# Two units' y side by side in 4-byte words: three transposes and one copy per pair, in a fused recurrence and MoE kernel

## The chip, the cores and the metric

The kernel runs on one core of one Trainium2 chip. The metric is the time of one execution on the device in microseconds; the time of before is 174.89 us, the median of three runs (174.61 to 177.36). Profiles are one execution each, taken by the hardware profiler; TensorE, VectorE, ScalarE, GpSimd and SyncE appear there as PE (its weight loads as PEld), DVE, ACT, POOL and SP.

## The reference

A gated linear recurrence over 768 steps for 4 batches of 8 heads of width 48, and then a two-layer SiLU network over its output, row by row (3072 tokens of 384 values, hidden width 2048). All inputs and the output are float32.

```python
f = 1.0 / (1.0 + np.exp(-f_logit))
for t in range(S):                                   # S = 768
    state = f[:, :, t, :, None] * state + np.einsum('bhd,bhe->bhde', k[:, :, t], v[:, :, t])
    y[:, :, t] = np.einsum('bhd,bhde->bhe', q[:, :, t], state)
x = y.transpose(0, 2, 1, 3).reshape(B * S, H * D)    # 3072 x 384
h = x @ w_in                                         # 384 x 2048
out = (h * (1.0 / (1.0 + np.exp(-h)))) @ w_out       # 2048 x 384
```

## The kernel before

The sequence of each batch is cut into six chunks of 128 steps. A unit is one chunk of one batch; two units make a pair, and there are 12 pairs (PAIRS). Pairs 0 to 3 (form T) take the first two chunks of one batch with the steps interleaved, pairs 4 to 11 (form N) take one chunk of two batches.

All work is written out by hand in one string, PLAN. A word such as `yT.0.1:P:2` is a step: its kind, the pair, the unit (or the piece), the engine that does it (P TensorE, V VectorE, A ScalarE, G GpSimd, S SyncE) and the buffer slots that it takes. The order of the words is the order in each engine's queue. There are 8 banks of PSUM (slots of class pb, 128 x 512 words each), 4 buffers xT, 3 buffers yb, and so on (SLOTS). A step waits for what it reads and for the last reader of the buffer that it takes.

For the change these steps matter, in the order of the data:

- `y` and `yi` (line 349, 459, 455): the recurrence's output of a unit, 128 steps x 384 values in float32, in a PSUM bank.
- `yc` (line 463): a cast of it to bf16 into yb. Helper `copy`, so the profile shows line 191 for ScalarE and line 193 for VectorE.
- `yT` (line 467): three 128 x 128 transposes on TensorE (a weight load of yb and a matmul with the identity) into one PSUM bank, in bf16. `qkc` and `tq` (line 412) do the like for q and k.
- `xc` (line 469): a copy of that bank into the unit's half of xT, which is 128 x 3 x 256 in bf16: 128 columns of unit 0 and then 128 of unit 1.
- `mi` (line 335): the first product of the network, w_in as weights and xT streamed, six matmuls per step. In pairs 0 and 1 a step takes one unit (128 columns); from pair 2 on a step takes both (256 columns).
- `si` (line 340): SiLU on ScalarE, from a PSUM bank of 2 x 2 x 128 words to hT in bf16.
- `mo` (line 370) and `ms` (line 273): the second product, the latter after seven-product sums of blocks (`hs`, `wt`, `ca`).

Pairs 5 to 11 use `yT` and `xc` for some units and, for the others, a DMA transpose (`yD`, line 471); the change does not touch them. w_in comes in four DMAs that GpSimd issues (`wi`, line 237), w_out in four more (`wo`).

Of the kernel before, what the change touches and what calls it, by code (L numbers as in the profile page):

```python
# [53 lines left out]
at.2.1.0:V:3 mo.0.0.1:P: f.5.0:S:2 at.2.1.1:V: mo.1.1.2:P: wt.6:V: k.4.1:S: d.2:P:7,4 y.2:P:6,5 su.2.0:V:0 mo.0.0.2:P: yc.2.0:A:1 vb.3.0:A:6
mo.1.0.2:P: vb.3.1:V:2 q.4.1:S:4 sd.2.1:V:1 yi.2.1:P: sc.3.1:P:3,6 yc.2.1:V:2 su.2.1:G:0 q.4.0:S: sc.3.0:P:7,4 mo.0.0.3:P: E.4.0:A: at.3.0.0:V:0
k.5.0:S:0 mo.1.0.3:P: at.3.1.0:V:1 L.4.0:A:1 yT.2.0:P:5 at.3.1.1:V: yT.2.1:P:7 v.4.0:S:4 mo.1.1.3:P: xc.2.1:A:2 at.3.0.1:V: oc.1.0:A:0 cs.4.1:P:3
v.5.0:S:0 cs.4.0:P:6 xc.2.0:V: oc.1.1:A: oc.0.0:V:1 d.3:P:7,4 a.4.1:A:1 y.3:P:0,5 q.5.0:S:0 su.3.0:V:0 al.4.1:A:4 ia.4.0:A:4 qg.4.1:G:3 mi.2.7:P:2
E.5.0:A: yc.3.0:V:0 v.6.1:S:1 mi.2.3:P:1 ia.4.1:A:2 sd.3.1:V:0 al.4.0:A:5 yi.3.1:P: a.4.0:A:3 yT.3.0:P:7 f.7.0:S:0 mi.2.1:P:0 su.3.1:G:0 L.5.0:A:2
xc.3.0:V:3 yc.3.1:V:1 mi.2.4:P:3 v.4.1:S: wt.4:V: yT.3.1:P:4 cs.5.0:P:6 mi.2.0:P:7 xc.3.1:V: ki.4.1:V: mi.2.5:P:5 si.2.0:A:2 vb.4.0:V:3 qkD.4.1:S:0
# [54 lines left out]
def kernel(  # L114
# [48 lines left out]
    w_in_sb = sb.tile([128, KT, d_ff], BF16, name="w_in_sb")  # L163
# [25 lines left out]
    def copy(eng, dst, src):
        if eng == "A":  # L190
            nc.scalar.copy(dst, src)  # L191
        else:
            ENG[eng].tensor_copy(dst, src)  # L193
# [38 lines left out]
    def emit(kind, rest, eng):  # L232
        if kind in ("wi", "wo"):
            n, parts = rest[0], count[kind]
# [93 lines left out]
        if kind == "mi":  # L328
            j = rest[1]
            h = at("h", P, j).rearrange("p (n c) -> p n c", n=2)  # L330
            for i in range(2):
                n = 2 * j + i
                cols = slice(rest[2] * C, (rest[2] + 1) * C) if len(rest) > 2 else slice(0, 2 * C)
                for kk in range(KT):
                    nc.tensor.matmul(h[:, i, cols], w_in_sb[:, kk, n * 128:(n + 1) * 128], at("xT", P)[:, kk, cols],  # L335
                                     start=(kk == 0), stop=(kk == KT - 1))
            return
        if kind == "si":
            j = rest[1]
            return nc.scalar.activation(at("hT", P).rearrange("p u n c -> p n u c")[:, 2 * j:2 * j + 2], at("h", P, j).rearrange("p (n u c) -> p n u c", n=2, u=2), AF.Silu)  # L340
# [24 lines left out]
        b, c = us[i]
        last = c == CHUNKS - 1
# [128 lines left out]
    def takes(kind, rest):  # L495
        if kind in ("wi", "wo", "wt", "so", "yi", "yj", "idle"):
            return []
        P = rest[0]
# [60 lines left out]
    with tc.manual_schedule():  # L559
# [67 lines left out]
```

## Time and profile before

| what | before |
|---|---|
| median of three runs | 174.89 us |
| span of the profiled execution | 173.4 us |
| median less that span | 1.49 us |
| instructions | 5477 |
| PE, PEld busy | 160.4 us, 141.5 us |
| ACT, DVE, POOL busy | 129.6 us, 121.3 us, 71.2 us |

The profile gives the span from the first to the last instruction; for the time of the profiled execution itself no other figure is given, and the median stands beside it. Times in a timeline count from the start of the span. A row of a group gives line, engine, operation, what is written and read, the shape, the count, then busy time and the mean of one in ns, then the idle time in front of it on its engine and what ended that. In a timeline or chain row the first two numbers are start and length in us, and xN is the number of instructions merged. Matmuls are pipelined: the length of one matmul row (219 ns) is not the distance to the next.

### The profile page before, as it was taken

The page shows a single profiled execution, that of the slowest core. Times are in us where ns is not written, and L with a number is a line of the kernel's source. Part 1 is how long each engine was busy: PE and PEld are TensorE (multiplying, and loading weights), DVE is VectorE, ACT ScalarE, POOL GpSimd, SP SyncE. Part 2 cuts the span into 40 slices and gives each one's busy share as a digit, 9 for nine tenths or more (in the row PEclk, how much of TensorE's full clock was granted, in tenths as well). Part 3 has the DMA queues.
Part 4 walks back from the last instruction along what each step waited for, and adds up shares of the span by engine and source line. Part 5 has one row for each costly group of instructions (what it writes and reads, how often), then busy time and mean ns, then how long its engine had stood idle before and what let it go on. Part 6 is the DMA issues. An engine that isn't in the chain of part 4 may idle for free.

```text
span 173.4 us, 5477 instructions
## 1 busy us (share of the span) xinstructions
PE 160.4 (92%) x2245; PEld 141.5 (82%) x2245; DVE 121.3 (70%) x234; ACT 129.6 (75%) x248; POOL 71.2 (41%) x115
## 2 busy tenths in 40 slices
PE   0687898999999999999999999999996999999993
PEld 0255698976789888999998999999895998999992
DVE  7188950039995997958899779989965677966050
ACT  3999697783989899999768798798955877603511
POOL 6059872930240147899946305202467201000300
PEclk9999999999999999999999999999999999999999
DMA  5999999999999999979999969896999795120305
GB/s 138 324 325 319 241 206 227 203 206 195 185 194 200 195 200 204 176 150 208 245 188 188 219 135 211 191 198 134 191 171 183 177 145 139 60 80 4 136 27 200
DMA packets 108695, 31.73 MB, mean 183 GB/s; under 512 B 102704, under 2 KB 108144, under 8 KB 108672
## 3 DMA queue, kind: packets, MB, share of 16 engines
q1 hardware_dynamic: 103936, 25.70, 71.7%
q0 software_dynamic: 4736, 5.70, 15.8%
q8 instruction: 17, 0.28, 0.6%
q14 instruction: 6, 0.05, 0.1%
HBM read 25.17 MB, written 4.72 MB: 172 GB/s over the span
## 4 chain that ended last, share of the span: by engine, by line
PE 69%; DMA 17%; POOL 4%; SPq 4%; ACT 3%; issue 1%; POOLq 0%
PE pb L335 28%; PE pb L273 22%; PE pb L370 7%; DMA w_in_sb<-in_moe_w_in_dram 6%; DMA w_out_sb<-in_moe_w_out_dram 5%; DMA qkT<-qk 4%; POOL qk L405 3%; DMA f<-in_f_logit_dram 2%; PE pb L438 2%; SPq L305 2%; PE pb L459 2%; PE pb L455 2%; PE pb L395 2%; SPq L424 1%; ACT x L400 1%
## 5 line engine op out<-in xcount | busy, mean ns | idle before, releaser
L335 PE MATMUL pb<-xT,w_in_sb 128*128 128x256 bf16 (+1 forms) x672 | 69.7, 257 | 0.5 <-DMA w_in_sb<-in_moe_w_in_dram 0.5
L340 ACT ACTIVATE hT<-pb 128x512 bf16<-128x512 f32 x96 | 51.9, 605 | 14.1 <-PE pb L335 13.4
L335 PEld LDWEIGHTS <-w_in_sb 128*128 128x128 bf16 x672 | 56.3, 98 | 5.9 <-DMA w_in_sb<-in_moe_w_in_dram 0.6
L273 PE MATMUL pb<-w_sum,hT 128*128 128x192 bf16 x288 | 28.0, 246 | 0.0
L405 POOL TENSOR_TENSOR qk<-q,x 128x384 bf16<-128x384 f32 x16 | 16.3, 1020 | 27.5 <-ACT x L400 12.4
L490 POOL TENSOR_TENSOR st<-sd,al 48x192 bf16<-48x192 f32 x32 | 16.9, 529 | 25.6 <-DVE sd L480 13.5
L400 ACT ACTIVATE x<-pb 128x384 f32<-128x384 f32 x48 | 22.2, 511 | 3.3 <-PE pb L395 2.7
L273 PEld LDWEIGHTS <-hT 128*128 128x128 bf16 x288 | 23.8, 98 | 0.6
L442 DVE TENSOR_TENSOR atm<-pb,triu 128x512 bf16<-128x512 f32 x32 | 20.5, 683 | 5.2 <-PE pb L438 5.0
L370 PE MATMUL pb<-w_out_sb,hT 128*128 128x384 bf16 (+1 forms) x128 | 17.7, 286 | 0.1
L593 ACT ACT_TABLE_LOAD x13 | 16.7, 1283 | 0.2
L405 POOL TENSOR_TENSOR qk<-k,x 128x384 bf16<-128x384 f32 x13 | 13.8, 1062 | 6.7 <-ACT x L400 5.4
L273 PE MATMUL pb<-w_out_sb,qkTT 128*128 128x192 bf16 x144 | 14.7, 246 | 0.0
L256 DVE TENSOR_TENSOR hT<-hT 128x1024 bf16<-128x1024 bf16 x18 | 14.6, 813 | 0.0
L382 POOL DMA_DIRECT2D out_dram<-ob x7 | 3.9, 565 | 24.6 <-ACT hT L340 24.6
L370 PEld LDWEIGHTS <-hT 128*128 128x128 bf16 x128 | 11.1, 98 | 3.6 <-issue 0.3
L191 ACT CAST yb<-pb 128x384 bf16<-128x384 f32 x15 | 7.3, 490 | 8.5 <-PE pb L349 4.8
L312 ACT ACTIVATE f<-f 128x768 f32<-128x768 f32 (+1 forms) x13 | 10.4, 809 | 2.4 <-DMA f<-in_f_logit_dram 2.2
L273 PEld LDWEIGHTS <-qkTT 128*128 128x128 bf16 x144 | 12.0, 98 | 0.3
L256 DVE TENSOR_TENSOR qkTT<-hT 128x2048 bf16<-128x2048 bf16 x9 | 11.1, 1233 | 1.2 <-ACT hT L340 1.2
L193 DVE COPY qkTT<-pb 128x1024 bf16<-128x1024 bf16 x4 | 2.8, 692 | 12.0 <-PE pb L412 12.0
L442 DVE TENSOR_TENSOR atm<-pb,mask 128x512 bf16<-128x512 f32 x16 | 10.0, 684 | 1.3 <-PE pb L434 1.3
(86 smaller groups left out, 235.6 us busy)
## 6 DMA issues: line engine op xcount, KB each, us to landing
f<-in_f_logit_dram SPq DMA_DIRECT2D x11, 384.0 KB, 4.8
k<-in_k_dram SPq DMA_DIRECT2D x16, 192.0 KB, 4.1
q<-in_q_dram SPq DMA_DIRECT2D x16, 192.0 KB, 3.7
v<-in_v_dram SPq DMA_DIRECT2D x16, 192.0 KB, 4.1
k<-in_k_dram SPq DMA_DIRECT2D x4, 384.0 KB, 4.9
q<-in_q_dram SPq DMA_DIRECT2D x4, 384.0 KB, 4.8
v<-in_v_dram SPq DMA_DIRECT2D x4, 384.0 KB, 10.7
w_in_sb<-in_moe_w_in_dram POOLq DMA_DIRECT2D x4, 384.0 KB, 8.8
```

The lines of the kernel that those rows point to most:

```text
L191: nc.scalar.copy(dst, src)
L256: return ENG[eng].tensor_tensor(out=h_sum(P, m), in0=x, in1=y, op=op)
L273: nc.tensor.matmul(at(BANK[m], P)[:, half * W:(half + 1) * W], x, w, start=first, stop=(n == KH - 1), skip_group_check=True)
L312: return nc.scalar.activation(e, at("f", P)[:, j * w:(j + 1) * w], AF.Exp, scale=-1.0)
L335: nc.tensor.matmul(h[:, i, cols], w_in_sb[:, kk, n * 128:(n + 1) * 128], at("xT", P)[:, kk, cols], start=(kk == 0), stop=(kk == KT - 1))
L340: return nc.scalar.activation(at("hT", P).rearrange("p u n c -> p n u c")[:, 2 * j:2 * j + 2], at("h", P, j).rearrange("p (n u c) -> p n u ...
L370: nc.tensor.matmul(at("o", P, i)[:, cols], at("hT", P)[:, i, n], w_out_sb[:, n, cols], start=(n == 0), stop=(n == NT - 1))
L400: nc.scalar.activation(at(kind, P, i).rearrange("p h d -> p (h d)"), at("cs", P, i)[:, 0:HD], AF.Exp, scale=1.0 if kind == "ia" else -1.0)
L405: ENG[eng].tensor_mul(at("qk", P, i)[:, j, :, 0:D], heads("qk"[j], P, i), at("ia" if j else "a", P, i))
L442: ENG[eng].tensor_mul(at("atm", P, i)[:, r], at(f"s{r}", P, i).rearrange("p (n c) -> p n c", c=C), mask[:, None, :].to_broadcast([C, NP, C]))
L490: ENG[eng].tensor_mul(at("st", P, i)[lo:lo + D, :, r * D:(r + 1) * D], src[lo:lo + D, :, r * D:(r + 1) * D], al_of(P, i)[lo:lo + D, :, Non ...
L593: nc.scalar.preload_act_table_set(TABLES[mode])
```

## The change

For pairs 0 to 4, in place of two `yc`, two `yT` and two `xc` there are two `yp`, one `yt` and one `xp`:

- `yp` casts a unit's y to bf16 straight into xT, at every second element: unit 0 at the even places and unit 1 at the odd ones. xT then holds 128 x 384 words of 4 bytes, each with one value of either unit.
- `yt` transposes xT, read as float32 words, in three 128 x 128 pieces with a float32 identity (`ident32`) into one PSUM bank.
- `xp` copies the 128 x 384 words back into the same xT. The columns of the two units now alternate.
- `mi` of pairs 0 and 1 reads every second column of xT; `mi` of pairs 2 to 4 reads all 256 as they lie, so that its result alternates too, and `si` of pairs 2 to 4 reads it with a step of two words. `si` of pairs 0 and 1 reads as before.

Engines: the casts stay where they were. The copy is on ScalarE in pairs 0 and 2 and on VectorE in pairs 1, 3 and 4. Before, ScalarE had one copy each in pairs 0, 2 and 4, and VectorE the other seven. `yt` stands in PLAN where the pair's second `yT` (for pair 0 the place between both) stood, and one bank per pair is taken less. The rest of PLAN is unchanged.

```diff
-... su.0.0:V:0 y.0:P:3,7 qg.2.1:G:0 yc.0.0:A:0
-at.1.0.1:V: yi.0.1:P: tq.2.0:P:0 al.3:A:3 yc.0.1:A:1 at.1.1.0:V: yT.0.0:P:3 a.3.0:A:2 yT.0.1:P:2 xc.0.0:A:0 ki.2.1:V: y.1:P:7,5 qkc.2.0:A:1
-mi.0.6.0:P:3 sd.0.1:V:1 yi.1.1:P: xc.0.1:V: yc.1.0:A:2 tq.2.1:P:1 ...
-yc.1.1:A:0 yT.1.0:P:2 mi.0.7.1:P: a.3.1:A:4 xc.1.0:V:1 mi.0.0.0:P:7 yT.1.1:P:4 wo.0:G: mi.1.7.0:P:1 xc.1.1:V: mi.0.0.1:P: ...
+... su.0.0:V:0 y.0:P:3,7 qg.2.1:G:0 yp.0.0:A:0
+at.1.0.1:V: yi.0.1:P: tq.2.0:P:0 al.3:A:3 yp.0.1:A: at.1.1.0:V: a.3.0:A:2 yt.0:P:2 xp.0:A: ki.2.1:V: y.1:P:7,5 qkc.2.0:A:1
+mi.0.6.0:P:3 sd.0.1:V:1 yi.1.1:P: yp.1.0:A:1 tq.2.1:P:1 ...
+yp.1.1:A: mi.0.7.1:P: a.3.1:A:4 mi.0.0.0:P:7 yt.1:P:4 xp.1:V: wo.0:G: mi.1.7.0:P:1 mi.0.0.1:P: ...
...
-yT.4.1:P:3 yc.4.0:A:0 sc.5.0:P:0,4 ... yT.4.0:P:1 xc.4.1:V:0 qg.5.1:G:1 ms.2.5:P:
-xc.4.0:A: cc.3:V:1 at.5.0.0:V:0 ...
+yp.4.0:A: sc.5.0:P:0,4 ... yt.4:P:1 xp.4:V: qg.5.1:G:1 ms.2.5:P:
+cc.3:V:1 at.5.0.0:V:0 ...
...
+    ident32 = sb.tile([C, C], F32, name="ident32")
...
+    by_unit = {("mi", *rest[:2]) for kind, rest, eng, got in plan if kind == "mi" and len(rest) > 2}
...
+    def mixed(P):
+
+        return ("yt", P) in names
...
                 cols = slice(rest[2] * C, (rest[2] + 1) * C) if len(rest) > 2 else slice(0, 2 * C)
+                xcols = slice(rest[2], 2 * C, 2) if len(rest) > 2 and mixed(P) else cols
                 for kk in range(KT):
-                    nc.tensor.matmul(h[:, i, cols], w_in_sb[:, kk, n * 128:(n + 1) * 128], at("xT", P)[:, kk, cols],
+                    nc.tensor.matmul(h[:, i, cols], w_in_sb[:, kk, n * 128:(n + 1) * 128], at("xT", P)[:, kk, xcols],
...
-            return nc.scalar.activation(at("hT", P).rearrange("p u n c -> p n u c")[:, 2 * j:2 * j + 2], at("h", P, j).rearrange("p (n u c) -> p n u c", n=2, u=2), AF.Silu)
+            if mixed(P) and ("mi", P, j) not in by_unit:
+                src = at("h", P, j).rearrange("p (n c u) -> p n u c", n=2, u=2)
+            else:
+                src = at("h", P, j).rearrange("p (n u c) -> p n u c", n=2, u=2)
+            return nc.scalar.activation(at("hT", P).rearrange("p u n c -> p n u c")[:, 2 * j:2 * j + 2], src, AF.Silu)
...
+        if kind == "yt":
+            both = at("xT", P).rearrange("p n c -> p (n c)").bitcast(F32)
+            for n in range(KT):
+                nc.tensor.transpose(at("yt", P)[:, n * C:(n + 1) * C], both[:, n * C:(n + 1) * C], ident32)
+            return
+        if kind == "xp":
+            return copy(eng, at("xT", P).rearrange("p n c -> p (n c)").bitcast(F32), at("yt", P)[:, 0:KT * C])
...
+        elif kind == "yp":
+            copy(eng, at("xT", P).rearrange("p n c -> p (n c)").rearrange("p (d i) -> p d i", i=2)[:, :, i], at("y", P, i)[:, 0:HD])
...
         make_identity(nc, ident)
+        make_identity(nc, ident32)
```

More of the change, by code (lines that the diff above doesn't have):

```diff
@@ L44 @@
 cs.2.1:P:3 qkc.0.1:V: wi.0:G: al.2:A:2 ia.2.0:A:0 sc.0.0:P:1,7 sc.0.1:P:4,6 vb.0.1:A:2 at.0.0.0:V:2 vb.0.0:G:3 L.3.0:A:0 wi.2:G: at.0.1.1:V:3
-d.0:P:0,1 ia.2.1:A:1 ki.2.0:G: at.0.1.0:V: cs.3.1:P:6 a.2.1:A:4 at.0.0.1:V: v.3.0:S:3 cs.3.0:P:4 wi.1:G: su.0.0:V:0 y.0:P:3,7 qg.2.1:G:0 yc.0.0:A:0
-at.1.0.1:V: yi.0.1:P: tq.2.0:P:0 al.3:A:3 yc.0.1:A:1 at.1.1.0:V: yT.0.0:P:3 a.3.0:A:2 yT.0.1:P:2 xc.0.0:A:0 ki.2.1:V: y.1:P:7,5 qkc.2.0:A:1
-mi.0.6.0:P:3 sd.0.1:V:1 yi.1.1:P: xc.0.1:V: yc.1.0:A:2 tq.2.1:P:1 su.0.1:G:0 ia.3.0:A:3 mi.0.6.1:P: qkc.2.1:V: ia.3.1:A:0 mi.0.7.0:P:0 su.1.1:G:0
-yc.1.1:A:0 yT.1.0:P:2 mi.0.7.1:P: a.3.1:A:4 xc.1.0:V:1 mi.0.0.0:P:7 yT.1.1:P:4 wo.0:G: mi.1.7.0:P:1 xc.1.1:V: mi.0.0.1:P: mi.1.6.0:P:5 wo.1:G:
+d.0:P:0,1 ia.2.1:A:1 ki.2.0:G: at.0.1.0:V: cs.3.1:P:6 a.2.1:A:4 at.0.0.1:V: v.3.0:S:3 cs.3.0:P:4 wi.1:G: su.0.0:V:0 y.0:P:3,7 qg.2.1:G:0 yp.0.0:A:0
+at.1.0.1:V: yi.0.1:P: tq.2.0:P:0 al.3:A:3 yp.0.1:A: at.1.1.0:V: a.3.0:A:2 yt.0:P:2 xp.0:A: ki.2.1:V: y.1:P:7,5 qkc.2.0:A:1
+mi.0.6.0:P:3 sd.0.1:V:1 yi.1.1:P: yp.1.0:A:1 tq.2.1:P:1 su.0.1:G:0 ia.3.0:A:3 mi.0.6.1:P: qkc.2.1:V: ia.3.1:A:0 mi.0.7.0:P:0 su.1.1:G:0
+yp.1.1:A: mi.0.7.1:P: a.3.1:A:4 mi.0.0.0:P:7 yt.1:P:4 xp.1:V: wo.0:G: mi.1.7.0:P:1 mi.0.0.1:P: mi.1.6.0:P:5 wo.1:G:
 mi.1.1.0:P:2 si.0.6:A:0 mi.1.0.1:P:6 f.4.0:S:1 mi.1.1.1:P: mi.0.4.0:P:4 si.1.1:A:1 si.0.0:A: mi.0.1.1:P:3 qg.3.1:G:1 mi.1.7.1:P: mi.0.1.0:P:
@@ L53 @@
 si.0.4:A: mo.1.1.0:P:2 qkc.3.0:V:0 si.1.6:A: tq.3.1:P:7 sc.2.0:P:6,4 qkc.3.1:A: sc.2.1:P:5,3 at.2.0.1:V:2 mo.1.1.1:P: at.2.0.0:V: mo.1.0.1:P:
[L54 to L59, printed above, removed]
+at.2.1.0:V:3 mo.0.0.1:P: f.5.0:S:2 at.2.1.1:V: mo.1.1.2:P: wt.6:V: k.4.1:S: d.2:P:7,4 y.2:P:6,5 su.2.0:V:0 mo.0.0.2:P: yp.2.0:A:2 vb.3.0:A:6
+mo.1.0.2:P: vb.3.1:V:2 q.4.1:S:4 sd.2.1:V:1 yi.2.1:P: sc.3.1:P:3,6 yp.2.1:V: su.2.1:G:0 q.4.0:S: sc.3.0:P:7,4 mo.0.0.3:P: E.4.0:A: at.3.0.0:V:0
+k.5.0:S:0 mo.1.0.3:P: at.3.1.0:V:1 L.4.0:A:1 at.3.1.1:V: yt.2:P:7 v.4.0:S:4 mo.1.1.3:P: xp.2:A: at.3.0.1:V: oc.1.0:A:0 cs.4.1:P:3
+v.5.0:S:0 cs.4.0:P:6 oc.1.1:A: oc.0.0:V:1 d.3:P:7,4 a.4.1:A:1 y.3:P:0,5 q.5.0:S:0 su.3.0:V:0 al.4.1:A:4 ia.4.0:A:4 qg.4.1:G:3 mi.2.7:P:2
+E.5.0:A: yp.3.0:V:3 v.6.1:S:1 mi.2.3:P:1 ia.4.1:A:2 sd.3.1:V:0 al.4.0:A:5 yi.3.1:P: a.4.0:A:3 f.7.0:S:0 mi.2.1:P:0 su.3.1:G:0 L.5.0:A:2
+yp.3.1:V: mi.2.4:P:3 v.4.1:S: wt.4:V: yt.3:P:4 cs.5.0:P:6 mi.2.0:P:7 xp.3:V: ki.4.1:V: mi.2.5:P:5 si.2.0:A:2 vb.4.0:V:3 qkD.4.1:S:0
 ki.4.0:V:0 mi.2.2:P:4 si.2.7:A: qg.4.0:V: si.2.1:A: mi.3.7:P:7 wt.3:V: si.2.5:A: mi.3.2:P:2 qkD.4.0:S:1 si.2.4:A: si.3.7:A:3 d.4.0:P:0 mi.2.6:P:5
@@ L64 @@
 al.5.0:A:1 mo.0.1.2:P: al.5.1:A:0 ia.5.1:A:1 qg.5.0:G:4 at.4.1.0:V: q.6.1:S: ia.5.0:A:2 ms.3.3:P:2 E.7.0:A: cc.2:V:0 ki.5.0:G: at.4.0.1:V: y.4.1:P:0
-f.8.0:S:2 L.7.0:A:0 ms.3.4:P: hs.2.6:V: yc.4.1:A:2 tq.5.0:P:6 k.6.0:S: a.5.1:A:4 y.4.0:P:1 qkc.5.0:V:3 E.6.0:A: mo.0.1.3:P: su.4.0:G:0 ca.2.0:V:
-yT.4.1:P:3 yc.4.0:A:0 sc.5.0:P:0,4 v.6.0:S: L.6.0:A:1 su.4.1:G:0 d.5.0:P:6 ms.2.2:P: sd.5.0:V:1 q.7.0:S:2 yT.4.0:P:1 xc.4.1:V:0 qg.5.1:G:1 ms.2.5:P:
-xc.4.0:A: cc.3:V:1 at.5.0.0:V:0 oc.0.1:A: v.5.1:S: cs.6.1:P:6 cs.7.0:P:3 a.6.1:A:3 ki.5.1:V: cs.6.0:P:1 ms.2.1:P:5 ia.6.1:A:0 ca.3.0:V: qkD.5.1:S:4
+f.8.0:S:2 L.7.0:A:0 ms.3.4:P: hs.2.6:V: yp.4.1:A:0 tq.5.0:P:6 k.6.0:S: a.5.1:A:4 y.4.0:P:1 qkc.5.0:V:3 E.6.0:A: mo.0.1.3:P: su.4.0:G:0 ca.2.0:V:
+yp.4.0:A: sc.5.0:P:0,4 v.6.0:S: L.6.0:A:1 su.4.1:G:0 d.5.0:P:6 ms.2.2:P: sd.5.0:V:1 q.7.0:S:2 yt.4:P:1 xp.4:V: qg.5.1:G:1 ms.2.5:P:
+cc.3:V:1 at.5.0.0:V:0 oc.0.1:A: v.5.1:S: cs.6.1:P:6 cs.7.0:P:3 a.6.1:A:3 ki.5.1:V: cs.6.0:P:1 ms.2.1:P:5 ia.6.1:A:0 ca.3.0:V: qkD.5.1:S:4
 qg.6.1:G:2 at.5.0.1:V: a.6.0:A:2 mi.4.6:P:0 al.6.1:A:2 al.6.0:A:3 oc.2:A:2 hs.3.5:V:0 y.5.0:P:6 a.7.0:A:4 ms.2.6:P:4 ia.7.0:A:1 al.7.0:A:5 E.8.0:A:
@@ L515, in takes @@
             return [("ob", P)]
+        if kind == "yt":
+            return [(kind, P)]
+        if kind in ("yp", "xp"):
+            return [("xT", P)]
         if kind in ("si", "xc", "yD"):
@@ L530, in takes @@
         return [({"ki": "qk", "qg": "qk", "yc": "yb", "su": "st"}.get(kind, kind), *rest[:2])]
-    cls_of = lambda kind: {"ia": "x", "a": "x", "cs": "pb", "tq": "pb", "y": "pb", "yT": "pb", "d": "pb", "o": "pb", "s0": "pb",
+    cls_of = lambda kind: {"ia": "x", "a": "x", "cs": "pb", "tq": "pb", "y": "pb", "yT": "pb", "yt": "pb", "d": "pb", "o": "pb", "s0": "pb",
                            "s1": "pb", "h": "pb", "oa": "pb", "ob2": "pb", "oc": "pb", "hE": "qkTT", "hF": "qkT"}.get(kind, kind)
```

## The prediction

> **What bounds the kernel now.** I read the page first: busy times, the forty slices, the chain that ended last. Rows of section 2 hold one digit per slice of 173.4 / 40 = 4.3 us.
>
> ```profile
> span 173.4 us, 5477 instructions
> PE 160.4 (92%) x2245; PEld 141.5 (82%) x2245; DVE 121.3 (70%) x234; ACT 129.6 (75%) x248; POOL 71.2 (41%) x115
> ...
> PE   0687898999999999999999999999996999999993
> ...
> ACT  3999697783989899999768798798955877603511
> ...
> PE 69%; DMA 17%; POOL 4%; SPq 4%; ACT 3%; issue 1%; POOLq 0%
> ```
>
> TensorE is full from the seventh slice to the end but for one dip, and the chain runs through it. The waits of TensorE alone, from 27 us on, and two stretches of the windows (columns: width, then busy us and count for PE, PEld, DVE, ACT, POOL, then granted clock, DMA share, GB/s) make that exact.
>
> ```profile
> PE pb L438 <- DMA qkT<-qk: 1.5, 1, 1.5
> PE pb L335 <- DMA w_in_sb<-in_moe_w_in_dram: 0.5, 1, 0.5
> 27.49:34.50 7.01, 7.01 (x126) 7.01 (x127) 0.00 (x0) 4.78 (x10) 4.65 (x6) 1.00 1.24 217
> 50.00:85.00 35.00, 35.00 (x469) 31.20 (x467) 28.11 (x49) 32.89 (x68) 20.77 (x30) 1.00 1.00 197
> ```
>
> After 27.49 us TensorE waits once, 1.5 us. A microsecond of ScalarE or VectorE saved there is worth nothing by itself; a microsecond of TensorE moves the end almost one for one. The second window is the stretch in which pairs 2 to 4 pass the first MoE product: ScalarE is busy 32.89 of 35.00 us there and has 2.11 us to spare. The clock is 1.00 throughout, so it explains nothing.
>
> **The prices.** Groups by line and shape (busy us, mean ns of one, idle before), and one row of the chain.
>
> ```profile
> L467 PE MATMUL pb<-ident,yb 128*128 128x128 bf16 x42 | 4.5, 219 | 0.0
> L467 PEld LDWEIGHTS <-yb 128*128 128x128 bf16 x42 | 3.1, 98 | 0.5 <-ACT yb L191 0.2
> L191 ACT CAST yb<-pb 128x384 bf16<-128x384 f32 x15 | 7.3, 490 | 8.5 <-PE pb L349 4.8 <-PE pb L459 3.5
> L191 ACT COPY xT<-pb 128x384 bf16<-128x384 bf16 x6 | 2.9, 482 | 2.2 <-PE pb L467 2.2
> L193 DVE COPY xT<-pb 128x384 bf16<-128x384 bf16 x8 | 2.8, 352 | 1.4 <-PE pb L467 1.3
> L191 ACT COPY ob<-pb 128x384 f32<-128x384 f32 x9 | 4.3, 485 | 0.0
> L193 DVE COPY ob<-pb 128x384 f32<-128x384 f32 x4 | 2.2, 547 | 0.0
> L191 ACT COPY ob<-pb 128x192 f32<-128x192 f32 x2 | 0.6, 319 | 4.7 <-PE pb L370 4.7
> L340 ACT ACTIVATE hT<-pb 128x512 bf16<-128x512 f32 x96 | 51.9, 605 | 14.1 <-PE pb L335 13.4
> ...
> 45.47 0.34 PE pb L467 x6
> ```
>
> **Turns (yT to yt).** Thirty of the 42 turns belong to pairs 0 to 4. In the chain six take 0.34 us, 57 ns each, so the change removes 30 x 57 = 1.71 us of TensorE and adds 15 turns of 4-byte words. No row shows such a turn. Low end: 57 ns, since it streams the same 128 columns and nothing suggests fewer; high end: a weight load and a turn one behind the other with no overlap, 98 + 219 = 317 ns. I take 98 ns, the weight load as the pace, the nearest row to a turn whose weights are twice as wide. Fifteen give 1.47 us; 57 ns would give 0.86 and 317 ns 4.76.
>
> **Copies (xc to xp).** Ten copies of bf16 become five of words. The nearest rows are the copies of ob, same 128x384 words: 485 ns on ScalarE, 547 on VectorE. VectorE loses 7 x 352 and gains 3 x 547; ScalarE loses 3 x 482 and gains 2 x 485. TensorE is the cover, so this is priced at nothing except where a copy is waited for, below. The casts (yp for yc) stay ten on the same engines, but write every second bf16. No row has such a write: between 0 and a doubled element time. ScalarE's 485 and 319 ns for 384 and 192 words give 0.865 ns a word, so 0.33 us more for one at worst. I take 0, as the elements read and written are as many as in the 490 ns row; the two on the start path leave 0.7 us for the range.
>
> **First MoE product.** Pairs 0 and 1 (192 matmuls of 128 columns) now stream every second bf16 of xT; pairs 2 to 4 stream 256 neighbours as before, but their SiLU (L340, 24 instructions) reads every second word of PSUM. Neither is in the trace. Matmuls: 7.01 / 126 = 55.6 ns now, between 0 and 55.6 ns more. SiLU: 605 ns now, between 0 and 512 x 0.865 = 443 ns more. I know no reason for a gain in either. I take 0 for both, the nearest rows being the same instructions with the same counts of elements, and carry the upper ends as rivals.
>
> **Set-up and queues.** The 4-byte identity adds a memset and a select to POOL. The 2-byte select took 0.29 us; double that for both is about 1.2 us. It is hidden under the 5.43 us in which POOL then waits:
>
> ```profile
> 3.63 0.29 POOL masks.py:199 TENSOR_SCALAR_AFFINE_SELECT ident<-ident 128x128 bf16<-128x128 bf16 x1
> 9.35 1.00 POOL L405 TENSOR_TENSOR qk<-k,x 128x384 bf16<-128x384 f32 x1 [5.43 <-ACT x L400]
> ```
>
> No DMA is added or moved on SP or POOL. xT is held from the cast on rather than from the copy on, but slot 0 comes to pair 4 long after pair 0's last product (34.5 us).
>
> **The added wait.** Before, unit 0's product waited for unit 0's copy; now it waits for both casts, the turns and the one copy. The timeline of the start:
>
> ```profile
> 20.80 0.48 ACT L191 CAST yb<-pb 128x384 bf16<-128x384 f32 x1
> 21.01 0.67 PE L467 MATMUL pb<-ident,yb 128*128 128x128 bf16 x6
> 21.33 0.17 PEld L467 LDWEIGHTS <-yb 128*128 128x128 bf16 x3 [0.17 <-ACT yb L191]
> 21.54 0.51 ACT L191 COPY xT<-pb 128x384 bf16<-128x384 bf16 x1
> 22.21 0.51 PE L335 MATMUL pb<-xT,w_in_sb 128*128 128x128 bf16 x6
> 23.92 0.57 ACT L191 CAST yb<-pb 128x384 bf16<-128x384 f32 x1
> 24.62 0.21 PEld L467 LDWEIGHTS <-yb 128*128 128x128 bf16 x3
> 24.68 0.33 PE L467 MATMUL pb<-ident,yb 128*128 128x128 bf16 x3
> 24.84 2.17 PE L335 MATMUL pb<-xT,w_in_sb 128*128 128x128 bf16 x36
> 25.11 0.36 DVE L193 COPY xT<-pb 128x384 bf16<-128x384 bf16 x1 [0.55 <-PE pb L467]
> 27.49 2.57 PEld L335 LDWEIGHTS <-w_in_sb 128*128 128x128 bf16 x46 [0.65 <-DMA w_in_sb<-in_moe_w_in_dram]
> ```
>
> Pair 0: unit 1's cast ends at 21.28 as before, the first word load starts at 21.33. The old turns ended at 21.68; three at 98 instead of 57 ns end 0.12 later, 21.80. The copy starts 0.10 later (as 25.11 follows the end at 25.01), 21.90 where the old one began at 21.54; its 0.485 us end at 22.39, and the first product starts near 22.45 instead of 22.21. Behind that copy on ScalarE stand the copy of qkTT and both casts of pair 1, all 0.36 us later.
>
> Pair 1 is where it hurts: its second cast ends at 23.92 + 0.36 + 0.57 = 24.85, the load follows at 24.90, the turns end 0.39 + 0.12 later at 25.41, VectorE's copy runs 25.51 to 26.06, and TensorE, whose next instruction is a product of pair 1, goes on at 26.13 instead of 24.84: 1.29 us late. What is late next is the weights' DMA: TensorE's loader stood 0.65 us before 27.49. So 1.29 - 0.65 = 0.64 us come through. VectorE has nothing else to do there (0.00 us busy in the first window).
>
> Pairs 2 to 4: 18 turns out, 9 in, 9 x 98 - 18 x 57 = -0.14 us. Pairs 2 and 3 have about 2 us of other TensorE work between turns and product. In pair 4 the copy on VectorE moves behind the turns:
>
> ```profile
> 68.21 0.35 DVE L193 COPY xT<-pb 128x384 bf16<-128x384 bf16 x1
> 70.07 0.68 DVE L442 TENSOR_TENSOR atm<-pb,triu 128x512 bf16<-128x512 f32 x1
> 71.23 0.36 PE L459 MATMUL pb<-vb,atm 128*128 128x48 bf16 x8
> ```
>
> It would start near 68.5 and take 0.2 us longer, so the copy of ct and the masks behind it come 0.5 us later; the mask that TensorE reads at 71.23 ended at 70.75, 0.48 us ahead. Cost about 0.
>
> **Sum.** +0.64 - 0.14 = +0.5 us on a span of 173.4, 173.9 us. The median of the runs is 174.89, 1.49 us above the span, which I put around it unchanged: **175.4 us**. Its own range: with 57 ns a turn and the start stall fully under the weights' DMA, -0.86 gives 174.0; with slow casts +0.7 gives 176.1.
>
> **Rivals.**
> - **A, slower: ScalarE becomes the bound in 50 to 85 us.** If the SiLU reads every second word at half pace, 24 x 443 ns = 10.6 us come onto an engine with 2.11 us to spare, plus the 0.48 us copy that it loses: 10.6 - 2.6 = 8.0 us, 183.4. It decides from 2.6 / 24 = 0.11 us more per SiLU. For it: ScalarE is near full there and TensorE needs its banks back. Against it: as many words are read, from one bank. The Trainium skill, Advanced Engine Details and Errata, PSUM Cachelines, says that PSUM lines are 8 bytes and every two consecutive elements should be contiguous for best throughput; it speaks of matmuls, and here the reader is ScalarE. No run yet shows it; by that rule the sum would be A's.
> - **B, slower: streaming every second bf16 halves TensorE's pace.** 66 matmuls before 27.49 and 126 after, 192 x 55.6 ns = 10.7 us, 186.1. For it: nothing covers them. Against it: four used elements still lie in every 16 bytes.
> - **C: the change isn't fewer turns in time.** If a turn of words costs 317 ns, pairs 2 to 4 get 9 x 0.317 - 1.03 = +1.83 us and the two turn sets of the start 6 x 0.219 = 1.31 more than in my sum: 0.64 + 1.31 + 1.83 = 3.8, 178.7. The Trainium skill, FP8 and Floating Point Precision, TensorE Precision Notes, counts four passes for true FP32, which at 57 ns a pass would be 228 ns a turn, between my value and C's; its TensorE: Matmul & The Clock Gate, Terms, calls the transpose mode four times faster for FP32, against it. No row here shows either.
> - **D, faster by over 2%** would need 3.5 us, more than all turns of the first five pairs (1.71 us).
>
> **How the numbers follow.** Forecast 0.60, A 0.20, B 0.11, C 0.06, D 0.03. A measurement of this kernel tells about 2%, 3.5 us, from no change: 171.4 to 178.4. The forecast and half of C lie within, 0.63; A, B and the other half of C are slower, 0.34; faster 0.03. The range runs from 174.0 to A's 183.4, rounded up to 184.0; it holds the forecast, C and most of A, and leaves out B and D.
>
> **What would show it.** Right: turns of words some 0.1 us apart; the SiLU of pairs 2 to 4 still near 605 ns; 55.6 ns between pair 0's matmuls; a TensorE gap of about 1 us near 25 us that ends on VectorE's copy, the wait for the weights gone. Wrong: SiLU at 0.7 us and more with TensorE waiting on it after 52 us (A), pair 0's and 1's matmuls 0.1 us apart (B), turns of 0.2 us or more (C).

## The result, and the profile after

| what | before | after |
|---|---|---|
| median of 20 runs each | 174.74 us | 175.25 us |
| fastest run | 173.52 us | 174.75 us |
| span of the profiled execution | 173.4 us | 174.5 us |
| time of that execution less its span | not given | 176.28 - 174.5 = 1.8 us |

The changed kernel takes 1.0058 times as long, with an interval of 1.0034 to 1.0083: 0.6 to 1.5 us more. That is inside what counts as no change here, but it is not nothing. The ratio leaves out runs more than 1.5% above a kernel's fastest (three of before, one of after) and so is not that of the medians of all 20, which is 1.0029, or 0.5 us.

The page of after, in the lines that answer to those shown of before:

```profile
span 174.5 us, 5446 instructions
PE 160.5 (92%) x2230; PEld 141.7 (81%) x2230; DVE 120.4 (69%) x230; ACT 129.7 (74%) x247; POOL 72.6 (42%) x117
...
PE   0677789999999999999999999999997999999993
...
PE 82%; DMA 6%; ACT 5%; POOL 2%; issue 2%; DVE 1%; SPq 1%; DVEq 0%
```

There are fifteen turns fewer, and TensorE is as busy as before (160.5 against 160.4 us). The digits of its fifth and sixth slice (17 to 26 us) fell from 8, 9 to 7, 8, and the dip of the seventh (8 before, 9 now) has moved ahead of it: the loss is at the start.

The waits of TensorE and the same two windows (columns as before):

```profile
PE pb L456 <- DMA qkT<-qk: 1.2, 1, 1.2
PE pb L342 <- DVE xT L195: 0.7, 1, 0.7
PE pb L430 <- DVE qk L423: 0.7, 1, 0.7
```

```profile
27.49:34.50 7.01, 7.01 (x125) 7.01 (x123) 0.00 (x0) 4.51 (x9) 5.02 (x6) 1.00 1.23 215
50.00:85.00 35.00, 35.00 (x463) 31.07 (x463) 27.64 (x49) 32.51 (x67) 20.81 (x28) 1.00 0.99 191
```

The wait for the weights w_in is gone, and a wait of 0.7 us for VectorE's copy into xT has taken its place. The wait for qk (0.2 us before) lies at 10.8 us, ahead of all that was changed, and is made good: TensorE's products at 20.4 us start 0.03 us apart in the two profiles. ScalarE in 50 to 85 us is no fuller than before (32.51 against 32.89 us).

The start in the timeline of after, with the rows of TensorE that matter behind it:

```profile
20.38 0.60 ACT L193 CAST xT<-pb 128x384 bf16<-128x384 f32 x1 [1.37 <-PE pb L360]
20.89 0.61 ACT L193 CAST xT<-pb 128x384 bf16<-128x384 f32 x1
21.55 0.55 PE L378 MATMUL pb<-ident,xT 128*128 128x128 f32 x3 [0.35 <-ACT xT L193]
22.18 0.48 ACT L193 COPY xT<-pb 128x384 f32<-128x384 f32 x1 [0.33 <-ACT x L418]
22.71 0.51 PE L342 MATMUL pb<-xT,w_in_sb 128*128 128x128 bf16 x6
23.46 0.61 ACT L193 CAST xT<-pb 128x384 bf16<-128x384 f32 x1
24.65 0.64 ACT L193 CAST xT<-pb 128x384 bf16<-128x384 f32 x1
25.34 0.55 PE L378 MATMUL pb<-ident,xT 128*128 128x128 f32 x3
25.99 0.56 DVE L195 COPY xT<-pb 128x384 f32<-128x384 f32 x1 [1.43 <-PE pb L378]
26.61 9.52 PE L342 MATMUL pb<-xT,w_in_sb 128*128 128x128 bf16 x162 [0.72 <-DVE xT L195]
35.97 1.46 PE L388 MATMUL pb<-w_out_sb,hT 128*128 128x384 bf16 x8
39.47 2.77 PE L388 MATMUL pb<-w_out_sb,hT 128*128 128x384 bf16 x16
48.91 1.48 PE L342 MATMUL pb<-xT,w_in_sb 128*128 128x256 bf16 x12
133.93 0.40 PE L456 MATMUL pb<-qkT 48*128 48x128 bf16 x8 [1.24 <-DMA qkT<-qk]
```

The same places in the timeline of before:

```profile
27.49 7.21 PE L335 MATMUL pb<-xT,w_in_sb 128*128 128x128 bf16 x126 [0.48 <-DMA w_in_sb<-in_moe_w_in_dram]
34.54 1.46 PE L370 MATMUL pb<-w_out_sb,hT 128*128 128x384 bf16 x8
38.05 3.02 PE L370 MATMUL pb<-w_out_sb,hT 128*128 128x384 bf16 x16
47.74 1.49 PE L335 MATMUL pb<-xT,w_in_sb 128*128 128x256 bf16 x12
132.88 0.40 PE L438 MATMUL pb<-qkT 48*128 48x128 bf16 x8 [1.47 <-DMA qkT<-qk]
```

Read the two against each other by the lag of after. The 126 products that start at 27.49 before are the last 126 of the 162 that start at 26.61. At (35.97 - 26.61) / 162 = 57.8 ns each they start at 28.69, so after is 1.20 us late there, and 35.97 - 34.54 = 1.43 us late when the second product begins. Then it gains 0.25 in sixteen products (2.77 for 3.02 us; in before the last three of their weight loads come after a gap of 0.32 us, at a place where e7 below waits for w_out) and is 1.17 late at the first product of 256 columns. It loses another 0.11 by 132 us, waits 0.23 less for the transposed qkT, and is 1.05 late from there to the end. More than all of the cost arises before 36 us.

Groups of after by shape (busy us, mean ns, idle before), and one row of the chain:

```profile
L193 ACT CAST xT<-pb 128x384 bf16<-128x384 f32 x7 | 4.1, 602 | 4.5 <-PE pb L360 4.5
L193 ACT CAST yb<-pb 128x384 bf16<-128x384 f32 x8 | 3.9, 481 | 3.8 <-PE pb L477 3.5
L195 DVE CAST xT<-pb 128x384 bf16<-128x384 f32 x3 | 1.8, 596 | 0.2 <-PE pb L473 0.2
L195 DVE CAST yb<-pb 128x384 bf16<-128x384 f32 x6 | 3.3, 552 | 3.8 <-PE pb L477 3.8
L195 DVE COPY xT<-pb 128x384 f32<-128x384 f32 x3 | 1.7, 558 | 2.0 <-PE pb L378 2.0
L193 ACT COPY xT<-pb 128x384 f32<-128x384 f32 x2 | 0.9, 474 | 0.3 <-ACT x L418 0.3
L351 ACT ACTIVATE hT<-pb 128x512 bf16<-128x512 f32 x96 | 51.9, 605 | 14.7 <-PE pb L342 14.0
...
46.65 0.33 PE pb L378 x3
```

The first two rows are one operation on one engine with one count of elements. Into xT, at every second bf16, it takes 602 ns; into yb, side by side, 481. VectorE's two rows below differ by less, 596 and 552.

### The profile page after: what moved, and what is told of

It is laid out like the page before. It is cut to its first block, busy times and chain, and to the rows that moved or that the text cites. A ratio compares the mean times of both kernels' runs of the same rounds, so it can differ in the third digit from the quotient of the medians.

```text
span 174.5 us, 5446 instructions
## 1 busy us (share of the span) xinstructions
PE 160.5 (92%) x2230; PEld 141.7 (81%) x2230; DVE 120.4 (69%) x230; ACT 129.7 (74%) x247; POOL 72.6 (42%) x117
## 4 chain that ended last, share of the span: by engine, by line
PE 82%; DMA 6%; ACT 5%; POOL 2%; issue 2%; DVE 1%; SPq 1%; DVEq 0%
PE pb L342 35%; PE pb L279 23%; PE pb L388 9%; DMA qkT<-qk 3%; PE pb L456 3%; DMA f<-in_f_logit_dram 2%; PE pb L477 2%; PE pb L473 2%; PE pb L413 2%; ACT x L418 2%; PE pb L430 1%; POOL qk L423 1%; ACT xT L193 1%; PE pb L496 1%; PE pb L378 1%
## 5 line engine op out<-in xcount | busy, mean ns | idle before, releaser
L510 POOL TENSOR_TENSOR st<-sd,al 48x192 bf16<-48x192 f32 x32 | 17.5, 547 | 27.1 <-DVE sd L500 13.4
L500 DVE TENSOR_TENSOR sd<-pb,st 128x384 f32<-128x384 f32 x16 | 8.8, 551 | 2.6 <-PE pb L496 2.5
```

The source lines that it names most:

```text
L500: nc.vector.tensor_add(at("sd", P, i), d_ps, prev_state(P, i))
L510: ENG[eng].tensor_mul(at("st", P, i)[lo:lo + D, :, r * D:(r + 1) * D], src[lo:lo + D, :, r * D:(r + 1) * D], al_of(P, i)[lo:lo + D, :, Non ...
```

## The experiments

Short diffs stand for the edits. "After" and "before" name the two kernels; each ratio is to the kernel before on the same chip.

**Which part costs: the start or the later pairs.** Two kernels take the change apart. `e1_old_start` has the old words of pairs 0 and 1 in after's PLAN, `e2_new_start` the old words of pairs 2 to 4.

```diff
 e1: -yp.0.0:A:0 ... yp.0.1:A: ... yt.0:P:2 xp.0:A: ... yp.1.0:A:1 ... yp.1.1:A: ... yt.1:P:4 xp.1:V:
     +yc.0.0:A:0 ... yT.0.0:P:3 ... xc.0.0:A:0 ... (the words of before, pairs 0 and 1)
 e2: -yp.2.0:A:2 ... yt.2:P:7 ... xp.2:A: ... (pairs 2, 3 and 4)
     +yc.2.0:A:1 ... yT.2.0:P:5 ... (the words of before)
```

> Pairs 0 and 1 go the old way (two casts to yb, six turns, two copies, unit 0's columns ahead of unit 1's); pairs 2 to 4 stay changed. Theory S (the cost sits in the start: pair 1's first product waits for both casts, the turns and the one copy, and the streaming of every second bf16 adds some 2 ns to each of 192 matmuls): the cost is gone, ratio to before 1.000 (0.998 to 1.002), pair 1's first product near 24.8 us and TensorE waits for w_in near 27.5 us as before. Rival W (the cost is in the words of all pairs: turns, SiLU with a step of two, VectorE's late copy in pair 4): more than half stays, 1.003 or more.

> Only pairs 0 and 1 are changed; pairs 2 to 4 go the old way. Theory S: all of the cost stays, ratio 1.006 (1.004 to 1.009), TensorE's gap of about 0.7 us ends on VectorE's copy near 26.6 us. Rival W: 1.003 or less.

Measured: e1 0.9982 (0.9945 to 1.0020), e2 1.0038 (1.0001 to 1.0076). With the old start TensorE waits for w_in again; with the new one alone it waits for the copy as in after. The waits of e1, and two rows of e2's timeline (its granted clock was 0.50 from 19 to 22 us and 1.00 where these rows lie, e4's below 0.83 from 130 to 140 us, so only distances in the start are read from these two):

```profile
PE pb L456 <- DMA qkT<-qk: 2.4, 1, 2.4
PE pb L342 <- DMA w_in_sb<-in_moe_w_in_dram: 0.5, 1, 0.5
```

```profile
25.21 0.63 ACT L193 CAST xT<-pb 128x384 bf16<-128x384 f32 x1
27.16 1.03 PE L342 MATMUL pb<-xT,w_in_sb 128*128 128x128 bf16 x15 [0.72 <-DVE xT L195]
```

In e2 the product follows the start of the second cast by 1.95 us, in after by 1.96. The cost of the change lies with pairs 0 and 1; pairs 2 to 4 alone show none that the interval tells from zero. e1's wait of 2.4 us for qkT shows something else. At the first product of 256 columns e1 is 1.35 us ahead of after (47.56 against 48.91); behind that wait only 0.23 is left (133.70 against 133.93).

**What in the start costs.** In `e4_casts_packed` the casts write the units one behind the other, in `e5_packed_stream` the products of pairs 0 and 1 stream neighbours. Both compute other numbers than the reference; what they keep is the work and its order.

```diff
 e4: -copy(eng, ... .rearrange("p (d i) -> p d i", i=2)[:, :, i], at("y", P, i)[:, 0:HD])
     +copy(eng, at("xT", P).rearrange("p n c -> p (n c)")[:, i * HD:(i + 1) * HD], at("y", P, i)[:, 0:HD])
 e5: -xcols = slice(rest[2], 2 * C, 2) if len(rest) > 2 and mixed(P) else cols
     +xcols = cols
```

> The casts write each unit's 384 bf16 side by side in one half of the buffer and no longer at every second place, so the words hold two neighbours of one unit (this changes what is computed; instructions, counts and waits stay). Theory S with the cast's writing as its widening: casts on ScalarE fall from 602 to about 490 ns, three of them lie on the path to pair 1's product, which comes 0.3 us earlier, ratio 1.004. Rival (602 ns comes from the engine's neighbours and not from the step of the write): 600 ns still, 1.006.

> The products of pairs 0 and 1 stream 128 neighbouring bf16 of xT and not every second one (this changes what is computed in these pairs; everything else stays). If the step costs the 2 ns that lie between the distances of these matmuls in the two profiles (57.8 against 55.7 ns): back to 55.7 ns, 192 x 2.1 = 0.4 us less, ratio 1.003 to 1.004. Rival (the distance is that of an early, colder stretch and not of the step): 57.8 ns still, 1.006.

Measured: e4 1.0026 (0.9986 to 1.0065), e5 1.0018 (0.9976 to 1.0060). Neither interval separates the kernel from after or from before, so the time settles neither; the rows do. A group and two rows of e4's timeline:

```profile
L193 ACT CAST xT<-pb 128x384 bf16<-128x384 f32 x7 | 3.4, 487 | 4.5 <-PE pb L360 4.5
```

```profile
20.27 0.48 ACT L193 CAST xT<-pb 128x384 bf16<-128x384 f32 x1 [1.36 <-PE pb L360]
25.91 1.26 PE L342 MATMUL pb<-xT,w_in_sb 128*128 128x128 bf16 x19 [0.72 <-DVE xT L195]
```

The step of two is what makes the cast slow: 487 ns without it, 602 with it. From the first cast to pair 1's product it takes 25.91 - 20.27 = 5.64 us here and 26.61 - 20.38 = 6.23 in after. The casts, with what queues behind them, are thus worth 0.59 us; the wait for the copy itself stays at 0.72, since it belongs to the new order. One row of e5's chain:

```profile
26.49 9.21 PE pb L342 x162
```

The same 162 products take 9.21 us from neighbours and 9.52 from every second element: 0.31 us, 1.9 ns each.

**What a turn of words costs.** `e6_turns_twice` makes every turn of pairs 2 to 4 twice.

```diff
-            for n in range(KT):
+            for n in [n for _ in range(2 if P > 1 else 1) for n in range(KT)]:
                 nc.tensor.transpose(at("yt", P)[:, n * C:(n + 1) * C], both[:, n * C:(n + 1) * C], ident32)
```

> The three turns of words are done twice in pairs 2, 3 and 4: nine turns more, in a stretch in which TensorE never waits. If a turn costs its 109 ns there and the end moves one for one: +0.98 us on the changed kernel, ratio 1.011 to 1.012. Rival (the turns hide, or the wait for the DMA near 132 us takes it up): 1.006. At 317 ns a turn, the upper end of the prediction: +2.9 us, 1.022.

Measured: 1.0130 (1.0076 to 1.0185), against 1.0058 for after. The chain of e6 where after has three turns in 0.33 us:

```profile
46.49 0.66 PE pb L378 x6
```

Six turns of words in 0.66 us are 110 ns each. From pair 1's product to a half set of scores at 132 us, rows of e6's timeline and the end of that stretch in after's:

```profile
26.45 9.52 PE L342 MATMUL pb<-xT,w_in_sb 128*128 128x128 bf16 x162 [0.72 <-DVE xT L195]
133.12 0.40 PE L456 MATMUL pb<-qkT 48*128 48x128 bf16 x8
```

```profile
132.30 0.40 PE L456 MATMUL pb<-qkT 48*128 48x128 bf16 x8
```

e6 takes 133.12 - 26.45 = 106.67 us and after 132.30 - 26.61 = 105.69: 0.98 us for nine turns, 109 ns each, so nothing hides them. By the times they cost some 0.0072 of 174.7 us, 1.3 us, uncertain by about 1 us.

**Can the start's loss be filled?** In `e3_filled`, after gets three product steps of pair 0 ahead of pair 1's first (and other banks where these need them). `e7_before_filled` does the like to before, against the wait for w_in.

```diff
 e3: -... mi.0.0.0:P:7 yt.1:P:4 xp.1:V: wo.0:G: mi.1.7.0:P:1 mi.0.0.1:P: mi.1.6.0:P:5 ...
     +... mi.0.0.0:P:7 mi.0.0.1:P: yt.1:P:4 xp.1:V: wo.0:G: mi.0.1.1:P:1 mi.0.1.0:P: mi.1.7.0:P:5 mi.1.6.0:P:2 ...
 e7: -... mi.1.1.1:P: mi.0.4.0:P:4 si.1.1:A:1 si.0.0:A: mi.0.1.1:P:3 qg.3.1:G:1 mi.1.7.1:P: mi.0.1.0:P:
     +... mi.1.1.1:P: mi.0.1.1:P:3 mi.1.7.1:P: mi.0.1.0:P: mi.0.4.0:P:4 si.1.1:A:1 si.0.0:A: qg.3.1:G:1
```

> The changed kernel with three products of pair 0 moved ahead: one in front of pair 1's turns, two between the turns and pair 1's first product, with the PSUM banks renamed from there on so that they find one free. Three steps of 0.35 us cover the 0.34 us in front of the turns and the 0.72 us behind them. Theory S: both gaps go, ratio 1.001 (0.999 to 1.003); what is left is the 2 ns a matmul, 0.4 us in all. Rival W, or a rival by which the start only shifts when the weights land: 1.005 or more.

> The kernel before with three products (mi.0.1.1, mi.1.7.1, mi.0.1.0) moved ahead of mi.0.4.0, where TensorE's loader stood 0.65 us for the third part of w_in; their weights are there already. If that wait reaches the end one for one: 0.5 to 0.65 us less, ratio 0.997 (0.995 to 0.998). Rival (later waits take it back, the DMA of qkT near 132 us first): 1.000.

Measured: e3 1.0002 (0.9964 to 1.0040), e7 1.0026 (0.9986 to 1.0065). The start of the second product in e3's timeline, and a row of its waits; then the same of e7:

```profile
34.95 1.46 PE L388 MATMUL pb<-w_out_sb,hT 128*128 128x384 bf16 x8
```

```profile
PE pb L456 <- DMA qkT<-qk: 2.6, 2, 2.2
```

```profile
33.85 1.48 PE L370 MATMUL pb<-w_out_sb,hT 128*128 128x384 bf16 x8
39.76 0.81 PE L370 MATMUL pb<-w_out_sb,hT 128*128 128x384 bf16 x4 [0.26 <-DMA w_out_sb<-in_moe_w_out_dram]
```

```profile
PE pb L438 <- DMA qkT<-qk: 2.4, 2, 1.5
```

e3 reaches the second product 1.02 us sooner than after: other work fills the new wait. By its times it costs nothing over before that can be told, though its interval still meets that of after (1.0034 to 1.0083). Its profiled execution doesn't keep the gain: it waits 2.6 us for qkT where after waited 1.2, and is 0.50 us behind after at the end of that wait (134.43 against 133.93). e7 reaches the second product 0.69 us sooner than before and is no faster; in its profile the gain comes back as waits for w_out and twice for qkT. Whether the earlier start makes these waits longer, or whether they only differ from one execution to the next, isn't settled by these runs.

**The wait for qkT near 132 us.** It was 1.5 us before, 1.2 after, 2.4 in e1. Theory D: it decides part of the end, and hides part of the change. `e8_before_other_order` and `e9_after_other_order` move the set that waits (sc.10.0) behind other work.

```diff
-... sc.10.1:P:0,3 xc.9.0:A: sc.10.0:P:7,6 q.11.0:S: at.10.1.1:V:2 ms.8.4:P: ... ms.7.7:P: ... cs.11.0:P:2 ... mi.9.3:P:3 ia.11.0:A:0 ... y.10.0:P:6 a.11.0:A:1 ... mi.9.1:P:7 ... y.10.1:P:0 ... mi.9.0:P:2
+... sc.10.1:P:0,3 xc.9.0:A: q.11.0:S: at.10.1.1:V:2 ... ms.8.4:P: ... ms.7.7:P: cs.11.0:P:2 sc.10.0:P:7,6 ... mi.9.3:P:3 y.10.1:P:0 mi.9.0:P:2 y.10.0:P:6 mi.9.1:P:7 ia.11.0:A:0 ... a.11.0:A:1
```

> The kernel before with another order of TensorE's work near 132 us: the half set of scores of pair 10 that waits for the DMA-transposed qkT (sc.10.0) stands behind three other pieces of work of pairs 7, 8 and 11, and two small sets move with it. Nothing is left out and nothing is computed otherwise. Theory D (the wait for qkT near 132 us, 1.5 us in the profile before, is time of the path that sets the end): the wait is gone or below 0.3 us and the ratio to the kernel before is 0.990 to 0.998. Rival (the same wait comes back at the next use of a DMA-transposed qkT, or the next set waits for an eviction): ratio 0.999 to 1.003 and as much waiting of TensorE in the sum.

> The kernel after with the same other order near 132 us as in the kernel before with another order. Theory D (the wait for qkT near 132 us takes up a part of the change's cost at the start): without that wait the change costs all that TensorE's stream lost, 1.2 to 1.3 us, so this ratio stands 0.007 above that of the kernel before with the other order. Rival (the cost measured is all there is): 0.004 to 0.006 above it.

Measured: e8 1.0018 (0.9985 to 1.0052), e9 1.0091 (1.0053 to 1.0130). The order was not as neutral as its text says: the two exponentials of pair 11 (ia, a) now come after the product that takes their bank, so pair 11's numbers are others, and ScalarE is late. A row of e8's timeline:

```profile
136.83 0.49 ACT L400 ACTIVATE x<-pb 128x384 f32<-128x384 f32 x1 [2.32 <-PE pb L335]
```

`e11_before_moved` and `e12_after_moved` put ia and a ahead of those products and leave the rest of that order.

```diff
-... mi.9.3:P:3 y.10.1:P:0 mi.9.0:P:2 y.10.0:P:6 mi.9.1:P:7 ia.11.0:A:0 so.6.1:G: cc.8:A:0 a.11.0:A:1 ...
+... ia.11.0:A:0 mi.9.3:P:3 a.11.0:A:1 cc.8:A:0 y.10.1:P:0 mi.9.0:P:2 y.10.0:P:6 mi.9.1:P:7 so.6.1:G: ...
```

> The kernel before with the same other order near 132 us, but with the two exponentials of pair 11 (ia.11.0 and a.11.0) ahead of the products of pair 9 that take their bank; in the run with the other order they stood behind them, read that bank after it was written again (so those outputs were other numbers), and ScalarE came late by some 2 us. Theory D: the qkT wait near 132 us is below 0.3 us, no new wait of more than 0.5 us stands in 130 to 142 us, and the ratio to the kernel before is 0.990 to 0.998. Rival (the time is given back at a later wait): 0.999 to 1.003, with another TensorE wait of about 1 us in the list.

> The kernel after with that same order. Theory D: 0.006 to 0.008 above the ratio of the kernel before with that order, that is 1.1 to 1.4 us, which is TensorE's own loss in the start. Rival (the wait takes up nothing of the change): 0.004 to 0.006 above it.

Measured: e11 1.0053 (1.0014 to 1.0092), e12 1.0070 (1.0038 to 1.0101). Rows of e11's timeline:

```profile
99.49 0.33 PE L455 MATMUL pb<-st,qkT 128*128 128x96 bf16 x4 [1.09 <-POOL st L490]
139.08 1.47 PE L335 MATMUL pb<-xT,w_in_sb 128*128 128x256 bf16 x12 [0.44 <-ACT hT L340]
165.79 5.11 PE L370 MATMUL pb<-w_out_sb,hT 128*128 128x192 bf16 x60
```

The wait for qkT is gone in all four, and by the times none is faster than its kernel without the move. The profiles say why in part. Take the stretch from the half set ahead of the wait (131.01 us in before, 132.30 in after) to the last 60 products (165.43 and 166.49). Before takes 34.42 us with a wait of 1.47, and after 34.19 with 1.24: less the wait, 32.95 in both, and 32.95 or 32.96 in e1, e3, e6, e7 and e10 too. So this wait reaches the end one for one, as the first half of theory D says, and between the profiles of before and after it hides 0.23 us of the change. But the new orders are longer by themselves: the stretch takes 33.66 us in e11 and e12 and 34.34 in e8 and e9, with no wait for qkT. Of what the wait gave back they lose 0.71 and 1.39 us, the 0.44 at 139.08 as one visible part. That leaves e11 0.76 us ahead of before in this stretch, and the wait of 1.09 us for POOL's state, ahead of the moved words, takes more than that. e12 is 0.57 us ahead of after at the last 60 products (165.92 against 166.49), which its times don't show. e2 and e8 show the wait for POOL's state as well and e12 doesn't, and why it comes is open. The distance that D gave between the two kernels came out as 0.0073 in one pair of runs and as 0.0017 in the other, each uncertain by about 0.004 to 0.005. That can't be told from the 0.0058 of the plain comparison.

**What lies outside the span.** `e10_before_ident32` adds the float32 identity to before, used by nothing.

```diff
+    ident32 = sb.tile([C, C], F32, name="ident32")
...
+        make_identity(nc, ident32)
```

> The kernel before with the float32 identity made in addition and used by nothing. If making it is what shortens the time outside of the profiled span in the kernels that hold it, the run's time less its span falls from 2.1 to about 1.8 us, the span grows by no more than 0.3 us and the ratio is 0.998 to 1.000. If it has nothing to do with that, the difference stays at 2.1 us and the ratio is 0.999 to 1.002.

Measured: 0.9971 (0.9921 to 1.0021), and run less span stays 2.1 us. The identity shows no cost and has nothing to do with the difference. The run is of use for another reason: its profiled span is 171.9 us, 1.5 less than that of before, with the same work on TensorE in the same order. Of its waits:

```profile
PE pb L439 <- DMA qkT<-qk: 0.3, 1, 0.3
```

Here TensorE waited 0.3 us for qkT, and 1.5 in the profile of before: nearly all of the difference. That wait differs between executions by as much as the whole effect of the change.

## Why the prediction was right or wrong

The forecast of 175.4 us and the measured 175.25 agree, and the mechanism was the forecast's. Some of the agreement is luck, as the terms show.

- **The start stall: right in place, too small.** The wait for w_in went, and the gap on VectorE's copy came. Pair 0's product came at 22.71 instead of 22.45, pair 1's at 26.61 instead of 26.13. The step that was mis-sized is "I take 0" for the casts: 602 ns instead of 490. Two of them delay pair 0 by 21.50 - 21.28 = 0.22 us (second cast's end after and before). Pair 0's turns add 0.06 to that, so its copy starts at 22.18 and not at 21.90, and pair 1's casts stand behind it: the slow first one brings the second to 24.65 in place of 24.28, and the second takes 0.64 for the 0.57 assumed. Of the 0.48 us missed, the casts make 0.22 + 0.09 + 0.07 = 0.38 and the turns of both pairs the other 0.10. The range carried 0.7 us for two slow casts, which holds that; it counted those of pair 0 alone, and those of pair 1 stand in the same queue ahead of the turns. (e4 puts the casts at 0.59, more than this 0.38: its start also beats the forecast's own rows, by 0.14 us, and why is not shown.)
- **Streaming every second bf16: "I take 0" was nearly right.** 57.8 ns against 55.6. It is 0.08 us from 26.61 to 28.69 and 0.23 in the 126 products behind. Rival B, half pace, is refuted.
- **Pairs 2 to 4: -0.14 us was wrong by a little.** A turn of words is 109 ns apart from the next, not 98, so nine cost 0.98 us and the eighteen old ones 1.03: 0.05 saved. Rival C (317 ns) is refuted. For its sentence on the Trainium skill's FP8 and Floating Point Precision, TensorE Precision Notes: four passes at 57 ns would be 228 ns, which the 109 of this trace doesn't show. The larger miss is the "Cost about 0" of pair 4's later copy on VectorE. Two rows of after, which answer to the last two that the prediction shows for pair 4:

```profile
71.79 0.68 DVE L460 TENSOR_TENSOR atm<-pb,triu 128x512 bf16<-128x512 f32 x1
72.38 0.49 PE L477 MATMUL pb<-vb,atm 128*128 128x48 bf16 x8
```

The mask now ends at 72.47, 0.09 us after the start of the eight products that read the unit's masks and not 0.48 us ahead, and they take 0.49 us instead of 0.36: 0.13 lost. In e1 and e6, whose pair 4 is changed, the same eight take 0.49 too, in e2, whose pair 4 is not, 0.36. This loss less the 0.05 is, within 0.03, the 0.11 us that after loses between 49 and 132 us.

- **SiLU with a step of two: 0, right.** 605 ns over all 96, before and after, 24 of them with the step. Rival A is refuted. The rule quoted from the Trainium skill, Advanced Engine Details and Errata, PSUM Cachelines, doesn't reach ScalarE's reading here: this trace has no loss to show for it.
- **Copies and set-up at nothing: right.** The word copies took 474 and 558 ns (485 and 547 assumed), and e10 shows no cost of the identity. Rival D (faster by over 2%) is refuted by the times.
- **"1.49 us above the span, which I put around it unchanged": wrong.** The span was that of one execution and the median that of others. In the further runs of before, run less span is 2.1 us, and in after's profiled execution 1.8. The profile of before was thus of a slower execution than the median, and the change took 0.3 us off what lies outside the span.

By its own profile the sum said +0.5 us of span, and the two profiles differ by 1.05: 0.48 for casts and turns in the start, 0.31 for streaming and 0.25 between the 0.14 that pairs 2 to 4 were to save and the 0.11 that they lose, less 0.25 in the sixteen products at 38 us and 0.23 of waiting for qkT. Less 0.3 outside of the span leaves 0.7 us, inside the measured 0.6 to 1.5. Against the profiled execution of after, 176.28 us, the forecast is 0.9 short; it meets the median because that lies 1.0 below the profiled execution.

What stays open: why the time outside the span is 2.1 us in before, e7, e10 and e11, 1.8 in after, e1, e3 to e6 and e9, and 1.9 in e2, e8 and e12. Neither the identity nor the new start alone explains it. Also open is why the fastest runs differ by 1.23 us and the medians by 0.51: the variable wait for qkT was the suspect. Without it the fastest runs of e12 and e11 still differ by 1.01 us and the medians by 0.11, while for e9 and e8 it is 0.98 and 1.10.

## What to carry to other kernels

Halving the number of transposes by packing two values into a word saves next to nothing where a turn of words takes nearly twice as long as a turn of halves, 109 ns for 57 here: count time, not instructions. What the packing does change is the order of dependence, since the first unit then waits for the second unit's cast; give the engine other work for that stretch, and price a strided write by a measured row. And before adding a microsecond that is won early to the end, compare the later waits for DMA, in more than one execution.

## What the runs showed of the hardware

- A transpose of 128 x 128 words of 4 bytes on TensorE takes 109 ns in a dense stretch (e6, nine more in 0.98 us), one of bf16 57 (the chain of before, six in 0.34 us).
- ScalarE's cast of 384 values from PSUM to bf16 in SBUF takes 0.12 us more when it writes every second element (602 ns for 481 to 490); VectorE's takes 596 ns into xT and 552 into yb (means of 3 and 6).
- TensorE streams 128 columns of bf16 with a step of two elements in 57.8 ns, neighbours in 55.6 (162 in 9.52 and 9.21 us, after and e5).
- ScalarE's SiLU reads 4-byte words in PSUM with a step of two at the pace of neighbours, 605 ns for 512 (mean of 96, before and after).
